# A gated recurrence ahead of a folded feed-forward block: the order of the opening transfers and jobs is written anew

## The chip, the core and the metric

The kernel runs on one core of one Trainium2 chip. The metric is the device time of one execution in microseconds (us); several executions of one kernel are summed up by their median. Inside the core five engines work side by side, each through its own queue in strict order: TensorE (PE in the profile), VectorE (DVE), ScalarE (ACT), GpSimd (POOL) and SyncE (SP). SP only issues transfers (DMA). PE writes to PSUM, a small memory of banks; the others read it there.

## The reference, cut to what matters

There are 4 sequences of 5824 tokens with 256 channels, 23296 tokens in all. A gated linear recurrence runs along each sequence, and its output goes through a feed-forward block that multiplies two projections.

```python
log_a = 8.0 * sigmoid(r_gate) * log(clip(sigmoid(a_param)))
a_t   = exp(log_a)
norm  = sqrt(maximum(1.0 - a_t * a_t, 1e-06))
h     = a_t[:, t] * h + norm * sigmoid(i_gate) * x      # along t; y[:, t] = h
a, b  = y @ w1, y @ w2                                  # 256 -> 1024 each
out   = ((a * b) @ w3) @ w_out                          # 1024 -> 1024 -> 256
```

The kernel folds w3 @ w_out once into one matrix of 1024 x 256 (`wp_sb`), since nothing lies between the two products.

## The kernel before, in words

The tokens are cut into 47 chunks: two of 256 tokens, 44 of 512 and one of 256. The two matrices of the up projections (w1, w2) and the folded matrix stay in SBUF. Every piece of work of a chunk is a named step, and the list `ORDER` gives all 2464 steps in one sequence; each step issues its instructions on one engine's queue. An engine takes its own steps in that order and waits, at each, until what the step reads is there and the buffer that it writes is free. So the list, and the sets that assign steps to engines, fix the schedule; there is no planner at run time.

The steps of chunk c, by letter, with the lines of the kernel before:

- `r c`, `i c`, `x c` load the three inputs (L136, on SP). `Lw1.k`, `Lw2.k`, `Lwo.k`, `Lw3.k` load a piece of 512 KB of a weight (L354, on SP) and `Cw...` casts it to bf16 (L361 to L363: POOL, or ACT and DVE for the members of `W_ACT` and `W_DVE`).
- `R c` and `I c` are the tanh of the two gates (L145 to L154, ACT). The sigmoids are computed from it. `p c` adds one (L159, POOL), `t c.half` multiplies by x (L175, L178).
- `V c` and `U c` turn the results so that channels lie on partitions. They are done by PE with 4 or 8 small transposes into PSUM (L185) for chunks in `TURN_R` and `TURN_U`, and by a transposing transfer on SP (L196) for the others.
- `d c.cb` is the exponential of one half of the channels (L207, ACT), `s c.cb` its square (L215, L217: ACT, DVE or POOL by set), `q c` the square root (L221, ACT). Root and exponential use different tables on ACT, so a change between them puts an ACT_TABLE_LOAD into ACT's queue.
- `g c` gates (L229 or L232, DVE), `h c.cb` is the scan along time (L249, DVE) and needs the chunk before, `y c` casts to bf16 (L258, POOL or ACT).
- `a c.mp.q` and `b c.mp` are the up projections of 128 and 256 hidden columns (L269, PE). `c c.mp.q` copies a from PSUM (L283 on DVE, L285 on ACT), `m c.mp` multiplies a and b (L297, DVE).
- `D c.j` is the folded down projection of 128 tokens (L308, PE), `e c.j2` copies it from PSUM, `o c.j2` stores it (L327, SP).
- `Ft`, `Fc`, `Fm`, `Fe` with an index 0 to 7 transpose a piece of w3, copy it, multiply it with w_out and copy the result to `wp_sb` (L368, L285 or L283, L379, L414 or L416). No `D` can begin before the last `Fe`.
- `W n` issues two matmuls on the identity matrix whose result nobody reads (L263, PE). There are 16 of them.

Buffers come from rings: `RINGS` gives the number of slots of each, and a step that takes a slot waits for the last reader of its former content. The PSUM ring "po" has 4 slots and serves `V`, `U`, `a`, `D`, `Ft` and `Fm`; the ring "pb" has 2 and serves `b` and `W`. Weight pieces are staged in the slots of the rings "a" and "nrm", 6 each, that also hold d's and s's results.

The transfers of SP run through one queue. In the trace at most eight of them are open: each has one of eight semaphores, and SP waits for the landing of the transfer that had it before.

The last 1961 of the 2464 steps stand in the same order before and after the change, so the change lies in the work up to about `b7.2`, the up projection of chunk 7.

Of the kernel before, what the change touches and what calls it, by code (L numbers as in the profile page):

```python
# [22 lines left out]
def kernel(  # L23
# [12 lines left out]
    nc = tc.nc  # L36
# [12 lines left out]
    CT = 512  # L49
    sizes = [256, 256] + [CT] * 44 + [256]  # L50
    assert sum(sizes) == NTOK
# [28 lines left out]
    TURN_R = {0, 1, 2, 3, 4, 7, 12}  # L80
    TURN_U = {0, 1, 2, 3, 4, 5, 6, 7}
    DV_TIMES = {0, 1}
    DV_PLUS = set()
    DV_HALF = {(2, 0)}
    DV_SQUARE = {(0, 0), (1, 0), (10, 0)}
    AC_SQUARE = {(1, 1), (2, 0), (2, 1), (3, 0), (4, 0), (4, 1), (6, 0), (8, 1), (9, 1), (11, 0), (11, 1), (12, 1),
        (13, 0), (13, 1), (14, 0), (14, 1), (15, 1)}
    DV_CAST = set()
    AC_CAST = {4}
    DV_COPY = {(0, 0, 0), (0, 1, 0), (0, 1, 1), (0, 3, 0), (1, 1, 0), (1, 1, 1), (1, 2, 0), (1, 2, 1), (1, 3, 0), (2,  # L90
        0, 1), (2, 1, 0), (2, 1, 1), (2, 3, 0), (3, 0, 1), (3, 2, 0), (3, 2, 1), (4, 0, 0), (4, 1, 0), (4, 2, 0), (4, 2,
        1), (5, 1, 1), (5, 2, 1), (6, 2, 0), (6, 2, 1), (6, 3, 1), (7, 0, 0), (7, 1, 1), (7, 3, 0), (7, 3, 1), (8, 1, 0),
        (8, 2, 0), (9, 1, 0), (9, 1, 1), (9, 2, 1), (10, 0, 0), (10, 1, 0), (10, 1, 1)}
    DV_EVAC = {(1, 0), (2, 0), (3, 1), (5, 1), (9, 0), (9, 1)}
    FOLD_ACT = {('c', 7), ('e', 0), ('e', 1), ('e', 2), ('e', 3), ('e', 7)}
    W_ACT = {('w2', 0), ('w3', 6)}
    W_DVE = {('w1', 1)}
    STAGE = {'w1': ['a', 'a'], 'w2': ['nrm', 'nrm'], 'wo': ['a', 'nrm'], 'w3': ['a', 'nrm', 'a', 'nrm', 'a', 'nrm',
        'a', 'nrm']}
    CASTING = set()  # L100
# [60 lines left out]
    def times(c, half):  # L161
        n = sizes[c] // P
        fused = c in DV_TIMES
        if half == 0 or fused:
            T["u", c] = ring(gates, [P, NCB, 4, P], BF16, name="u_t", tag="u")
# [34 lines left out]
    def decay(c, cb):  # L200
        w = sizes[c]
        if cb == 0:
            T["a", c] = ring(held, [P, NCB, CT], F32, name="a_t", tag="a")
        a, pr = T["a", c][:, cb, :w], T["pr", c][:, cb, :w]
        if long_rows(c):
            a, pr = in_time(a), turned(pr)
        nc.scalar.activation(out=a, in_=pr, func=AF.Exp, scale=la4[:, cb:cb + 1], bias=la4[:, cb:cb + 1])  # L207

    def square(c, cb):
        w = sizes[c]  # L210
        if cb == 0:
            T["n", c] = ring(held, [P, NCB, CT], F32, name="nrm", tag="nrm")
        n, a = T["n", c][:, cb, :w], T["a", c][:, cb, :w]
        if (c, cb) in AC_SQUARE:
            nc.scalar.activation(out=n, in_=a, func=AF.Square)  # L215
        else:
            (nc.vector if (c, cb) in DV_SQUARE else nc.gpsimd).tensor_mul(out=n, in0=a, in1=a)  # L217

# [17 lines left out]
    def scan(c, cb):  # L236
        w = sizes[c]
        if cb == 0:
            T["h", c] = ring(ypool, [P, NCB, CT], F32, name="h_t", tag="h")
        h, a, n = (T[key, c][:, :, :w] for key in "han")  # L240
        if cb == 0:
            for b in range(1, B):
                if 0 < b * S - starts[c] < w:
                    nc.vector.memset(a[:, :, b * S - starts[c]:b * S - starts[c] + 1], 0.0)
# [42 lines left out]
    def copy(c, mp, q):  # L287
        w = sizes[c]
        if q == 0:
            T["sa", c, mp] = ring(ffn, [P, 2, CT], BF16, name="sa", tag="sa")  # L290
        copy_to((c, mp, q) in DV_COPY, T["sa", c, mp][:, q, :w], T["pa", c, mp, q][:, :w])

    def product(c, mp):
        w = sizes[c]
        if mp == 0:
            T["g", c] = ring(ffn, [P, KD, CT], BF16, name="g_t", tag="g")
        nc.vector.tensor_mul(out=T["g", c][:, 2 * mp:2 * mp + 2, :w], in0=T["sa", c, mp][:, :, :w],  # L297
                             in1=T["pb", c, mp][:, :, :w])

    def down(c, j):  # L300
        if c == NCH - 1:
            T["po_last", j] = po = ring(psum_o, [P, D], F32, name="po", tag="po")
        else:
            if j % 2 == 0:
                T["po", c, j // 2] = ring(psum_o, [P, 2, D], F32, name="po", tag="po")
# [19 lines left out]
    def store(c, j2):  # L325
        t0 = starts[c] + 2 * j2 * P
        nc.sync.dma_start(out=out[t0:t0 + 2 * P, :].rearrange("(j p) c -> p j c", p=P),  # L327
                          in_=T["ot", c, j2])

# [88 lines left out]
    def last(c):  # L418
# [20 lines left out]
    ORDER = """  # L439
        r0 r1 E A3. A0. A1. i1 R1 R0 W3 V1 I1 V0 W13 W12 A2. W9 d1.0 d1.1 s1.0 i0 W15 I0 x0 t0.1 W14 d0.0 s0.0 s1.1  # L440
        d0.1 s0.1 q0 x1 t1.1 Lw1.0 r3 Lw2.0 r2 q1 R3 Lw1.1 i2 W11 U0 g0 h0.0 Lw2.1 Cw1.0 W10 W2 U1 W0 W7 R2 W4 h0.1
        Lw3.2 x2 g1 y0 W8 Lwo.0 Cw2.0 a0.1.0 a0.1.1 h1.0 c0.1.0 h1.1 a0.0.0 a0.0.1 V2 c0.1.1 d2.0 c0.0.0 W6 y1 b0.0
        c0.0.1 d2.1 I2 Cw1.1 a1.0.1 a1.0.0 b0.1 a1.1.0 a0.2.0 c1.0.0 c1.0.1 Cw2.1 p2 a0.2.1 Cw3.2 m0.0 m0.1 c1.1.0
        Lwo.1 b1.0 m1.0 t2.0 r4 W1 c0.2.0 a1.1.1 a0.3.0 t2.1 Cwo.0 W5 c1.1.1 Ft2 c0.2.1 a1.3.0 s2.0 b1.1 c0.3.0 b0.2
        U2 a1.3.1 s2.1 Cwo.1 i3 Fc2 V3 x3 Lw3.0 q2 Lw3.1 i4 Lw3.4 m1.1 c1.3.0 Fm2 R4 g2 h2.0 h2.1 d3.0 Lw3.7 c1.3.1
        m0.2 d3.1 Lw3.5 Fe2 a1.2.0 a0.3.1 b1.2 a1.2.1 I3 c0.3.1 V4 s3.0 d4.0 d4.1 b0.3 y2 c1.2.0 Cw3.0 c1.2.1 m1.2
        a2.0.0 a2.1.0 b1.3 m0.3 a2.2.0 b2.0 m1.3 a2.2.1 c2.0.0 Lw3.3 a2.0.1 s4.0 c2.2.0 s3.1 p3 t3.0 c2.1.0 Cw3.1 Ft0
        c2.0.1 c2.2.1 Fc0 m2.0 Cw3.4 b2.1 I4 s4.1 q4 r7 t3.1 a2.3.0 a2.1.1 Fm0 b2.2 p4 Cw3.5 c2.1.1 Ft4 c2.3.0 m2.1
        Fe0 Ft1 a2.3.1 U3 Lw3.6 q3 Fc4 c2.3.1 Fc1 Fm4 Cw3.7 b2.3 Ft5 g3 Fe4 Fc5 Ft7 x4 Cw3.3 R7 r5 h3.0 h3.1 Fm1 Fm5
        Fc7 Fe5 Ft3 Fm7 Fe1 Cw3.6 V7 Fe7 y3 Ft6 Fc3 d7.0 d7.1 Fc6 m2.2 Fm3 i6 r6 a3.1.0 Fe3 R5 Fm6 a3.1.1 c3.1.0  # L450
        c3.1.1 t4.0 Fe6 t4.1 i7 i5 x5 U4 a3.0.0 R6 D0.0 a3.0.1 D0.1 I6 c3.0.0 e0.0 m2.3 g4 a3.3.0 a3.2.0 b3.0 h4.0
        h4.1 b3.1 c3.0.1 m3.0 D1.0 a3.3.1 D1.1 I5 c3.3.0 y4 V5 r8 m3.1 a3.2.1 V6 b3.2 I7 e1.0 c3.2.0 c3.2.1 c3.3.1
        b3.3 m3.2 m3.3 p5 a4.0.1 r9 a4.1.0 d5.0 d5.1 R8 d6.0 s6.0 s7.0 d6.1 p6 t5.0 p7 x6 x7 o0.0 a4.0.0 i10 V8 D2.0
        D2.1 c4.0.0 c4.1.0 b4.0 r10 o1.0 s5.0 s5.1 R9 s6.1 c4.0.1 s7.1 e2.0 m4.0 a4.2.0 a4.2.1 q7 V9 c4.2.0 a4.1.1
        c4.2.1 b4.1 t5.1 b4.2 c4.1.1 U5 a4.3.0 i8 o2.0 m4.1 D3.0 r11 t6.0 t6.1 U6 q5 q6 g5 h5.0 h5.1 c4.3.0 m4.2 i9 g6
        d8.0 a4.3.1 D3.1 D2.2 D2.3 b4.3 c4.3.1 d9.0 e3.0 y5 a5.1.0 t7.0 s8.0 b5.0 m4.3 e2.1 R10 d8.1 a5.0.0 a5.0.1
        h6.0 h6.1 a5.2.0 c5.1.0 D4.0 c5.0.0 c5.0.1 I8 m5.0 x8 a5.1.1 D4.1 c5.2.0 o3.0 I9 b5.1 a5.2.1 c5.1.1 b5.2 m5.1
        c5.2.1 R11 e4.0 p8 y6 m5.2 r12 I10 t7.1 a5.3.0 a6.0.0 U7 V10 c5.3.0 c6.0.0 d9.1 x10 r13 D3.2 g7 D3.3 e3.1
        a6.0.1 x9 t8.0 t8.1 a6.1.0 d10.0 d10.1 o2.1 V11 a6.1.1 a5.3.1 h7.0 h7.1 s9.0 c6.0.1 s9.1 c6.1.0 b6.0 R13 o4.0
        a6.2.1 a6.2.0 c5.3.1 c6.1.1 y7 m6.0 b5.3 s8.1 U8 D4.2 b6.1 a7.0.0 p9 p10 m5.3 t9.0 c6.2.0 b6.2 c6.2.1 R12 m6.1  # L460
        a6.3.0 q8 q9 D4.3 a6.3.1 c7.0.0 m6.2 c6.3.0 e4.1 t9.1 b6.3 c6.3.1 t10.0 t10.1 m6.3 V12 a7.0.1 g8 x11 h8.0 h8.1
        b7.0 a7.1.0 s10.0 d12.0 d12.1 c7.1.0 c7.0.1 D6.0 D6.1 m7.0 a7.2.0 D5.0 a7.1.1 D5.1 V13 d13.0 s13.0 i11 I11
        e6.0 o3.1 d11.0 y8 d11.1 e5.0 r15 c7.1.1 a7.2.1 b7.1 c7.2.0 c7.2.1 b7.2 U9 U10 i13 i12 r14 o4.1 x13 d13.1 o6.0
        a7.3.0 a7.3.1 a8.0.1 o5.0 m7.1 m7.2 R15 I13 a8.0.0 c8.0.0 b7.3 c8.0.1 c7.3.0 D6.2 c7.3.1 m7.3 p11 b8.1 s11.0
        D6.3 b8.0 a8.1.0 D5.2 D5.3 g9 h9.0 s10.1 s12.0 t11.0 i16 s11.1 R14 h9.1 e6.1 I12 c8.1.0 q10 p13 a8.1.1 c8.1.1
        m8.0 V15 q11 p12 y9 e5.1 m8.1 a8.3.0 D7.0 D7.1 V14 i15 o5.1 o6.1 r16 t13.0 t11.1 U11 r19 x12 a8.2.0 c8.2.0 g10
        h10.0 h10.1 c8.3.0 e7.0 y10 a8.2.1 d15.0 r17 b8.2 a8.3.1 b9.0 a9.0.0 c8.2.1 t13.1 m8.2 o7.0 x15 s15.0 a9.0.1
# [142 lines left out]
```

## Time and profile before

| what | value |
|---|---|
| time, median of 3 executions | 514.76 us (514.51 to 515.69) |
| profiled execution, its own time | 514.32 us |
| its span, first to last instruction | 512.4 us |
| PE, ACT, DVE, POOL busy | 500.2, 465.6, 428.0, 312.8 us |
| last PE work ends, by the timeline | about 509.3 us |
| first `a` matmul (chunk 0) | 14.01 us |
| first `a` matmul of chunk 2 | 28.35 us |
| granted TensorE clock over the span | 1.00 |

A row of the timeline reads: start, duration, engine, line, operation, output and inputs, shape, how many, and in brackets how long the engine had been idle and who ended that. Matmuls overlap, so the rate of PE is read from start to start: 512 columns take 216 ns, 256 take 109 ns and 128 take 56 ns in the steady part of this trace. For the other engines too the distance from start to start of a run of instructions is a little smaller than one's duration.

### The profile page before, as it was taken

The numbers are of one execution on the slowest core, as the hardware profiler recorded it, in microseconds if no ns is written. First come the engines' busy times: TensorE is split into PE (matmuls) and PEld (weight loads), VectorE is DVE, ScalarE is ACT, GpSimd is POOL, SyncE is SP. The second block draws the span as 40 slices with busy tenths as digits, with TensorE's granted clock in tenths as the row PEclk, the third lists the DMA queues.
The fourth block names the chain that finished last, engine by engine and source line by source line (L and its number), as shares of the span: only waits on it lengthen the run. The fifth ranks groups of instructions, "written<-read, shape, count | busy, mean of one in ns | idle before, by whom it ended". The sixth has DMA issues, their size and how long they took to land.

```text
span 512.4 us, 8840 instructions
## 1 busy us (share of the span) xinstructions
PE 500.2 (98%) x3171; PEld 308.7 (60%) x3225; DVE 428.0 (84%) x414; ACT 465.6 (91%) x720; POOL 312.8 (61%) x271
## 2 busy tenths in 40 slices
PE   7899999999999999999999999999999999999997
PEld 3667565665565566556666556565566655656566
DVE  4899999999999879878878799878878697959762
ACT  7999999999999999999999999998998979888543
POOL 2683958546638945966685983957647569580200
PEclk9999999999999999999999999999999999999999
DMA  8998999999999998797999995898695895253112
GB/s 301 409 415 264 326 320 265 263 290 318 319 230 278 276 291 265 191 323 151 294 287 306 276 302 156 238 229 248 186 266 138 240 299 158 101 156 71 57 57 104
DMA packets 177280, 123.80 MB, mean 242 GB/s; under 512 B 86354, under 2 KB 172884, under 8 KB 177236
## 3 DMA queue, kind: packets, MB, share of 16 engines
q1 hardware_dynamic: 177232, 123.23, 84.1%
q8 instruction: 25, 0.41, 0.3%
q14 instruction: 19, 0.16, 0.1%
q10 hardware_dynamic: 4, 0.00, 0.0%
HBM read 78.91 MB, written 23.86 MB: 201 GB/s over the span
## 4 chain that ended last, share of the span: by engine, by line
PE 90%; ACT 4%; DMA 3%; issue 1%; SPq 1%; DVE 1%; ACTq 0%; DVEq 0%
PE po L308 30%; PE pb L269 29%; PE pa L269 28%; DMA r_t<-in_r_gate_dram 2%; DMA i_t<-in_i_gate_dram 1%; PE pw L379 1%; ACT sa L285 1%; PE ptr L185 1%; SPq L136 1%; PE ptw L368 1%; DVE h_t L249 0%; ACT th_r L145 0%; ACT a_t L207 0%; ACT ot L285 0%; ACT L154 0%
## 5 line engine op out<-in xcount | busy, mean ns | idle before, releaser
L297 DVE TENSOR_TENSOR g_t<-sa,pb 128x1024 bf16<-128x1024 bf16 (+1 forms) x188 | 218.9, 1181 | 63.0 <-PE pb L269 30.0
L269 PEld LDWEIGHTS <-w_sb 128*128 128x128 bf16 x1504 | 146.2, 98 | 146.9 <-issue 4.7
L285 ACT CAST sa<-pa 128x512 bf16<-128x512 f32 (+1 forms) x339 | 182.5, 588 | 26.7 <-PE pa L269 18.4
L269 PE MATMUL pa<-y_t,w_sb 128*128 128x512 bf16 (+1 forms) x721 | 185.8, 372 | 3.5 <-ACT sa L285 2.5
L269 PE MATMUL pb<-y_t,w_sb 128*128 128x512 bf16 (+1 forms) x729 | 182.5, 372 | 1.5
L308 PE MATMUL po<-wp_sb,g_t 128*128 128x256 bf16 x1456 | 177.7, 273 | 0.3
L308 PEld LDWEIGHTS <-g_t 128*128 128x128 bf16 x1456 | 142.4, 98 | 40.2 <-issue 0.5
L258 POOL CAST y_t<-h_t 128x1024 bf16<-128x1024 f32 (+1 forms) x46 | 51.1, 1112 | 142.1 <-DVE h_t L249 142.1
L178 POOL TENSOR_TENSOR u_t<-i_t,x_t 128x512 bf16<-128x512 f32 (+1 forms) x89 | 120.5, 1371 | 3.8 <-issue 1.7
L249 DVE TENSOR_TENSOR_SCAN h_t<-a_t,h_t,nrm 128x512 f32<-128x512 f32 (+1 forms) x92 | 119.7, 1331 | 1.9
L217 POOL TENSOR_TENSOR nrm<-a_t 128x512 f32<-128x512 f32 (+1 forms) x74 | 80.9, 1111 | 13.6 <-ACT a_t L207 10.7
L207 ACT ACTIVATE a_t<-rt,la 128x512 f32<-128x512 bf16 (+1 forms) x80 | 64.2, 821 | 0.0
L159 POOL TENSOR_SCALAR i_t<-i_t 128x1024 f32<-128x1024 f32 (+1 forms) x45 | 53.1, 1184 | 18.0 <-ACT i_t L154 18.0
L285 ACT COPY ot<-po 128x512 f32<-128x512 f32 (+1 forms) x85 | 49.6, 590 | 12.3 <-PE po L308 12.0
L232 DVE SCALAR_TENSOR_TENSOR nrm<-nrm,ut 128x1024 f32<-128x1024 f32 (+1 forms) x39 | 53.4, 1370 | 5.2 <-ACT nrm L221 5.2
L154 ACT ACTIVATE i_t<-i_t 128x1024 f32<-128x1024 f32 (+1 forms) x47 | 49.2, 1049 | 0.4 <-DMA i_t<-in_i_gate_dram 0.4
L221 ACT ACTIVATE nrm<-nrm 128x1024 f32<-128x1024 f32 (+1 forms) x47 | 48.3, 1040 | 0.2
L147 ACT ACTIVATE th_r<-r_t 128x1024 bf16<-128x1024 f32 (+1 forms) x40 | 42.6, 1065 | 0.0
L283 DVE CAST sa<-pa 128x512 bf16<-128x512 f32 (+1 forms) x37 | 21.8, 617 | 1.1 <-PE pa L269 0.9
L221 ACT ACT_TABLE_LOAD x17 | 21.8, 1283 | 0.3
L263 PE MATMUL warm<-ident 128*128 128x512 bf16 x32 | 11.1, 490 | 0.0
L215 ACT ACTIVATE nrm<-a_t 128x512 f32<-128x512 f32 (+1 forms) x17 | 10.7, 649 | 0.1
(57 smaller groups left out, 126.8 us busy)
## 6 DMA issues: line engine op xcount, KB each, us to landing
out_dram<-ot SPq DMA_DIRECT2D x90, 256.0 KB, 3.5
r_t<-in_r_gate_dram SPq DMA_DIRECT2D x44, 512.0 KB, 5.2
i_t<-in_i_gate_dram SPq DMA_DIRECT2D x44, 512.0 KB, 5.5
x_t<-in_x_dram SPq DMA_DIRECT2D x44, 512.0 KB, 5.3
wf<-in_moe_w_dram SPq DMA_DIRECT2D x12, 512.0 KB, 10.1
wf<-in_moe_w_out_dram SPq DMA_DIRECT2D x2, 512.0 KB, 10.3
r_t<-in_r_gate_dram SPq DMA_DIRECT2D x3, 256.0 KB, 2.9
i_t<-in_i_gate_dram SPq DMA_DIRECT2D x3, 256.0 KB, 4.1
```

The costliest lines, as they stand in the source:

```text
L159: (nc.vector if c in DV_PLUS else nc.gpsimd).tensor_scalar(t, t, 1.0, 1.0, op0=ALU.add, op1=ALU.mult)
L178: (nc.vector if (c, half) in DV_HALF else nc.gpsimd).tensor_mul(out=u, in0=t, in1=xt)
L207: nc.scalar.activation(out=a, in_=pr, func=AF.Exp, scale=la4[:, cb:cb + 1], bias=la4[:, cb:cb + 1])
L217: (nc.vector if (c, cb) in DV_SQUARE else nc.gpsimd).tensor_mul(out=n, in0=a, in1=a)
L221: nc.scalar.activation(out=T["n", c][:, :, :w], in_=T["n", c][:, :, :w], func=AF.Sqrt, scale=-1.0, bias=1.0)
L232: nc.vector.scalar_tensor_tensor(out=T["n", c][:, :, :w], in0=T["n", c][:, :, :w], scalar=1e-3, in1=T["pu", c][:, :, :w], op0=ALU.max, op1 ...
L249: nc.vector.tensor_tensor_scan(h[:, cb, :], a[:, cb, :], n[:, cb, :], init, ALU.mult, ALU.add)
L258: eng.tensor_copy(out=T["y", c][:, :, :w], in_=T["h", c][:, :, :w])
L269: nc.tensor.matmul(out=dst[:, :w], lhsT=w_sb[:, cb, m * P:(m + 1) * P], rhs=T["y", c][:, cb, :w], start=(cb == 0), stop=(cb == NCB - 1))
L285: nc.scalar.copy(out=dst, in_=src_ps)
L297: nc.vector.tensor_mul(out=T["g", c][:, 2 * mp:2 * mp + 2, :w], in0=T["sa", c, mp][:, :, :w], in1=T["pb", c, mp][:, :, :w])
L308: nc.tensor.matmul(out=po, lhsT=T["g", c][:, k, j * P:(j + 1) * P], rhs=wp_sb[:, k, :], start=(k == 0), stop=(k == KD - 1), skip_group_che ...
```

## The change: what it does

All steps stay, none is added; 503 of them are put in another order, some change the engine.

- Transfers: the opening order `r0 r1 i1 i0 x0 x1` becomes `r1 i0 r0 x0 i1 x1`. Then `Lw1.0 r3 Lw2.0 r2 Lw1.1 i2 Lw2.1 Lw3.2 x2` becomes `Lw1.0 r2 i2 Lw2.0 r3 Lw1.1 x2 Lw2.1 Lw3.2`.
- `U6` leaves `TURN_U`: PE's 8 transposes of chunk 6 become one transposing transfer on SP.
- Up to `b7.2`, ACT has 11 copies (`c`) fewer and DVE 11 more; one cast of y goes from ACT to POOL; `t2.0` from DVE to POOL; the casts of `w1.1`, `w2.0`, `w2.1`, `wo.0`, `w3.1` and `w3.6` change engine among ACT, DVE and POOL. Squares and fold copies move singly.
- The steps `W` stand elsewhere. Ahead of the first `a` of chunk 0 there were 13, now 12; between `U1` and that `a` there were 4, now 8.
- The helpers no longer assume that half 0 of a pair comes first: the first to arrive takes the buffer. This changes no instruction. `store` and `evac` take the width of a pair from a new helper, with the same result for every chunk that uses them.

```diff
     TURN_R = {0, 1, 2, 3, 4, 7, 12}
-    TURN_U = {0, 1, 2, 3, 4, 5, 6, 7}
+    TURN_U = {0, 1, 2, 3, 4, 5, 7}
     DV_TIMES = {0, 1}
-    DV_HALF = {(2, 0)}
-    DV_SQUARE = {(0, 0), (1, 0), (10, 0)}
+    DV_HALF = set()
+    DV_SQUARE = {(0, 0), (0, 1), (1, 1), (10, 0)}
...
-    AC_CAST = {4}
+    AC_CAST = set()
...
-    W_ACT = {('w2', 0), ('w3', 6)}
-    W_DVE = {('w1', 1)}
+    W_ACT = {('w2', 1), ('w3', 1), ('wo', 0)}
+    W_DVE = {('w2', 0)}
...
-        r0 r1 E A3. A0. A1. i1 R1 R0 W3 V1 I1 V0 W13 W12 A2. W9 d1.0 d1.1 s1.0 i0 W15 I0 x0 t0.1 W14 d0.0 s0.0 s1.1
-        d0.1 s0.1 q0 x1 t1.1 Lw1.0 r3 Lw2.0 r2 q1 R3 Lw1.1 i2 W11 U0 g0 h0.0 Lw2.1 Cw1.0 W10 W2 U1 W0 W7 R2 W4 h0.1
-        Lw3.2 x2 g1 y0 W8 Lwo.0 Cw2.0 a0.1.0 a0.1.1 h1.0 c0.1.0 h1.1 a0.0.0 a0.0.1 V2 c0.1.1 d2.0 c0.0.0 W6 y1 b0.0
...
+        A3. r1 i0 r0 x0 i1 x1 E A0. A1. A2. R1 I0 R0 W10 W13 V1 V0 W2 d1.0 d1.1 d0.0 s1.0 t0.1 s1.1 s0.0 d0.1 I1 t1.1
+        s0.1 q0 W14 U0 U1 W6 W11 W8 W3 W9 W1 W0 q1 W5 g0 h0.0 h0.1 g1 h1.0 Lw1.0 Cw1.0 y0 a0.0.1 c0.0.1 h1.1 r2 i2 R2
+        Lw2.0 Cw2.0 V2 a0.1.0 W12 a0.1.1 a0.0.0 W15 r3 Lw1.1 x2 Lw2.1 I2 d2.0 d2.1 y1 s2.1 p2 s2.0 R3 q2 Cw1.1 t2.0
+        t2.1 Cw2.1 c0.1.0 c0.1.1 b0.1 c0.0.0 m0.1 a1.1.1 a1.0.1 b0.0 a1.0.0 a1.1.0 b1.1 c1.1.1 m0.0 c1.0.1 c1.1.0
+        c1.0.0 m1.1 b1.0 a0.2.1 c0.2.1 a0.2.0 c0.2.0 a1.2.0 a1.3.1 c1.2.0 m1.0 a1.2.1 c1.3.1 c1.2.1 b0.2 m0.2 V3 U2
+        Lw3.2 Cw3.2 a0.3.0 Ft2 Lwo.1 Cwo.1 r4 Lwo.0 Lw3.4 Lw3.0 i3 Lw3.1 Lw3.7 x3 d3.1 d3.0 Fc2 R4 g2 c0.3.0 h2.1 h2.0
+        Cwo.0 W7 W4 a0.3.1 b1.2 b1.3 a1.3.0 V4 Fm2 y2 m1.2 Lw3.3 Lw3.5 Lw3.6 r7 i4 r5 r6 x4 i5 i6 b0.3 d4.1 s3.1 Fe2
...
     def times(c, half):
...
-        if half == 0 or fused:
+        if ("u", c) not in T:
             T["u", c] = ring(gates, [P, NCB, 4, P], BF16, name="u_t", tag="u")
```

## The prediction

> **What bounds the kernel now.** I read the page first: its busy times, its slices and the chain that ended last.
>
> ```profile
> PE 500.2 (98%) x3171; PEld 308.7 (60%) x3225; DVE 428.0 (84%) x414; ACT 465.6 (91%) x720; POOL 312.8 (61%) x271
> ...
> PE   7899999999999999999999999999999999999997
> ...
> PE 90%; ACT 4%; DMA 3%; issue 1%; SPq 1%; DVE 1%; ACTq 0%; DVEq 0%
> ```
>
> PE is on the chain for 90% of the span, and only the first slices lie below 9. Then I took the timeline of PE, which shows how the first 30 us are spent.
>
> ```profile
> 5.68 5.33 PE L263 MATMUL warm<-ident 128*128 128x512 bf16 x12
> 10.80 0.43 PE L185 MATMUL ptr<-ident,u_t 128*128 128x128 bf16 x4
> 11.07 1.03 PE L263 MATMUL warm<-ident 128*128 128x512 bf16 x4
> ...
> 14.01 1.03 PE L269 MATMUL pa<-y_t,w_sb 128*128 128x256 bf16 x8
> ...
> 18.95 0.38 PE L269 MATMUL pa<-y_t,w_sb 128*128 128x256 bf16 x2 [1.10 <-ACT sa L285]
> ...
> 26.50 0.38 PE L269 MATMUL pa<-y_t,w_sb 128*128 128x256 bf16 x2 [1.24 <-ACT sa L285]
> ```
>
> Three things are to be seen. The first real work starts at 14.01. Up to 26.5 there are two waits (1.10 and 1.24) and three more `W` steps. And the clock matters: 12 warm matmuls take 5.33, 0.427 each from start to start; after 10.89 four take 1.03 with the last one's tail, 0.216 each. From 28.6 to the end the starts of the matmuls follow one another without a gap over 0.2 us that isn't just a missing record. So nothing can be won behind 28.6 except PE work itself. What can be won is in the opening.
>
> The stretches show how near the other engines are to full there (PE, PEld, DVE, ACT, POOL).
>
> ```profile
> 10.00:30.00 20.00, 17.43 (x145) 11.83 (x145) 17.04 (x31) 19.61 (x30) 11.69 (x12) 1.00 1.04 412
> 30.00:50.00 20.00, 19.89 (x188) 14.99 (x188) 17.89 (x25) 18.88 (x27) 13.21 (x13) 1.00 0.96 336
> 50.00:98.80 48.80, 48.48 (x315) 29.89 (x320) 47.49 (x51) 48.52 (x69) 34.26 (x31) 1.00 1.08 285
> ```
>
> **What the Trainium skill says.** (1) "TensorE: Matmul & The Clock Gate", Part 1: PE begins at half clock and gets the full one after a window of about 3.4 us of sustained work; the window runs freely, so the moment differs between executions. The trace agrees: half speed until 10.89, 5.2 us after the steady work began at 5.68. (2) "ScalarE: Activation LUTs", What ACT_TABLE_LOAD costs: 1283 ns plus a drain. Here the load takes 1.28 and the next instruction starts 1.30 after it (8.89 to 10.19). (3) "SBUF — State Buffer", SBUF: two separate sides: a DVE instruction with two SBUF inputs and a GpSimd instruction shut each other out. The trace has a sign of it: `t2.1` on POOL took 1.71 beside `t2.0` on DVE, later ones 1.27. (4) "DMA: Bandwidth & Descriptors", Where 436 GB/s comes from: a ceiling of 435 GB/s. In the trace the landings of 512 KB follow each other every 1.25 to 1.36 us up to 44 us, 420 GB/s at best, in the order of issue. So a landing is known from the place in the order.
>
> **Part 1, the first transfers and ACT.** The landings in the trace are 3.28, 4.05, 5.58, 6.23, 6.87 and 7.52; the new order puts r1, i0, r0, x0, i1, x1 on them. ACT: R1 at 3.30, I0 at 4.07, R0 at 5.61, then from start to start 0.5 for R and 0.45 for each of four exponentials (6.14, 1.00 for two, less the tail): I1 starts at 7.92 and ends at 8.54. Table load 1.30, so q0 runs from 9.86 to 10.43 (before: 10.19). Both squares of chunk 0 are now on DVE, the second behind `t1.1` (8.56 to 9.25), ending at 9.7, in time. `g0` before started at 11.34, because `U0` sat behind 12 half-speed warm matmuls until 11.2. Now `U0` is done at 8.8, and `g0` starts at 10.46. Gating and scans took 11.34 to 13.28, the cast of y 0.06 + 0.62: y0 is ready at 13.08 instead of 13.96, a gain of 0.88 if PE is free.
>
> **Part 2, the warm matmuls.** PE is not free. `U1` needs `t1.1` and ends at 9.72; behind it stand 8 `W` steps, 16 matmuls, before `a0.0.1`. At full clock they take 16 x 0.216 = 3.46 and end at 13.18; at half clock 16 x 0.427 = 6.83 and end at 16.55. If the clock opens at O, the end is O + (16 - (O - 9.72)/0.427) x 0.216. Steady work begins at 6.27 (`V0`), with one gap of 0.5 before `U1`. If the gap is forgiven, O lies in 9.7 to 13.1 (3.4 to 6.8 after the start); if not, in 12.7 to 16.1. O = 10.89 gives 13.75, 12.7 gives 14.65, 14.3 gives 15.44. I take 14.7 for the start of `a0.0.1`, against 14.01: **a loss of 0.7**. DVE waits with it, since its copy `c0.0.1` now stands ahead of `h1.1`, `Cw2.0` and with them of y1 and the first b; ACT waits too, since `V2` follows `a0.0.1` and `d2.0` needs it.
>
> **Part 3, from there to chunk 2.** In the new order DVE has no hole between `c0.0.1` and the end of `h2.0`: 14 copies of 256 columns x 0.33, one scan 0.64, the weight cast 0.65, 5 products x 0.62, two gatings 1.19, two scans 2.45 = 12.65 (all from start to start of the rows of before). It starts 0.4 after `a0.0.1`, y2 adds 1.1: `a2.0.0` comes 14.2 after `a0.0.1`. The other chain, POOL's `s2.1`, `p2`, `Cw1.1` (three x 1.04) and `t2.0`, `t2.1` (two x 1.27) from the end of `d2.1`, ends within 0.2 of it. In the kernel before `a2.0.0` stood at 28.35, with `b1.3` (0.44) still to do, which the new order has done by then, and a gap of 0.23: comparable 29.0, 15.0 after its first `a`. **Gain 0.8**: the two waits and the `W` steps of before, of which the new order keeps a part. x2 lands at 17.7 instead of 20.2, but `t2.0` is behind `Cw1.1` on POOL until about 19 and is slower there than on DVE; the earlier landing alone is worth nothing.
>
> **Part 4, U6.** Eight transposes leave PE: 8 x 0.056 = **0.45 gained**, as PE is dense there. The transfer is issued behind the store `o2.1` on SP, at about 67; transposes landed about 5 us after their issue (46.72 to 51.59). `g6` needs it at about 73. Should it be late, `h6` and then chunk 6 wait, a us per us.
>
> **Part 5, the balance up to b7.2.** DVE gets 11 copies more (7 of 256 columns), less single items: 3.0 us more; ACT 2.3 less. Before, DVE had in the stretch from 10 to 98.8 6.4 idle, ACT 1.8. So DVE has 3 to 4 left, which is enough on average, but every `m` frees one of two "pb" slots and every copy one of four "po" slots, and PE waits where one is late. From below nothing, from above what a queue without slack lost at the start, 1.2. I take **a loss of 0.4**.
>
> **Sum** against the profiled execution (514.32, span 512.4): -0.7 + 0.8 + 0.45 - 0.4 = 0.15 faster, span 512.25, time 514.2. The median shown, 514.76, lies 0.44 above that execution, and its clock may have opened early; I add half of it: **514.4 us**.
>
> **The likeliest (0.46)**: within 0.2% (about 1.03 us, what a measurement can tell from no change), 513.7 to 515.8. **Rival, faster (0.28)**: the clock opens as early as before, at 10.9 or sooner, the start is at 13.75 or below, and the slots hold: 0.26 + 0.8 + 0.45 - 0.2 = 1.3 faster, 513.2. For it speaks that in the new order PE would be busy for 86% of 7.48 to 10.89, the window that opened the clock before; against it that the kernel before was busy for about 76% of 4.07 to 7.48, one window earlier, and the clock stayed at half. **Rival, slower (0.15)**: the clock opens only when the 16 warm matmuls are nearly through, and the start is at 16.5: -2.5 + 0.8 + 0.45 - 0.4 = 1.7 slower, 516.2. It decides from a start of about 15.9, an opening at 15.2. **Rival, slower (0.11)**: DVE, with 3.0 more, is the bound between 28 and 57, and PE waits there for 1.5 or more: 515.8. That the earlier landings change nothing is part of the likeliest.
>
> The range that holds 8 in 10 is 512.8 to 516.4: the low end is an early clock and no stall (1.5 gained), the high end a late clock with 0.4 of stalls and the median above its profile. Chances: faster 0.28, same 0.46, slower 0.26.
>
> **What would show it.** Part 1: `g0` near 10.5 and the cast of y near 12.5. Part 2: the spacing of the 16 warm matmuls, 0.427 or 0.216, and the first `a` at 14.7, later than 14.01. Part 3: `a2.0.0` near 28.9. Part 4: no `U6` on PE and `g6` not waiting. Part 5: PE without gaps from there, DVE above 17.9 busy in 30 to 50. I am wrong if the first `a` is at 13.1, if r0 in the third place lands well before 5.58, or if PE shows waits for DVE behind 30.

## The result, and the profile after

The changed kernel takes 517.97 us (median of 15 executions, 515.96 to 519.65); on the same chip the kernel before takes 515.65 (15 executions, 514.51 to 516.51). The ratio is **1.0047, 95% interval 1.0034 to 1.0061: slower**. The forecast was no change, 514.4, with a range up to 516.4. The profiled execution takes 516.24, the fourth quickest of the 15, with a span of 514.4, 2.0 more span than before.

The page of the changed kernel, busy times, PE's slices and the chain that ended last:

```profile
PE 499.7 (97%) x3163; PEld 308.2 (60%) x3217; DVE 433.4 (84%) x423; ACT 464.7 (90%) x712; POOL 313.6 (61%) x270
...
PE   7899989999999999999999999999999999999997
```

PE has 0.5 us less to do, as the 8 transposes of chunk 6 promised, but one slice has fallen to 8, the sixth, from 64 to 77 us. On the chain that ended last PE holds 76% where it held 90%, and ACT 12% where it held 4%. So the loss is behind the opening, where I expected nothing but 0.4. The stretch from 62 to 80 us says the same; first of the kernel before (start:end, length, then PE, PEld, DVE, ACT, POOL busy, clock, share and GB/s of DMA):

```profile
62.00:80.00 18.00, 17.95 (x134) 12.01 (x133) 17.71 (x19) 17.97 (x26) 12.03 (x12) 1.00 1.05 323
```

then of the changed kernel:

```profile
62.00:80.00 18.00, 16.25 (x118) 11.14 (x119) 16.29 (x18) 16.35 (x25) 8.93 (x9) 1.00 1.14 290
```

All four engines lose 1.4 to 3.1 us in the same stretch, so none of them is full there. The waits of the changed kernel between 60 and 125 us (engine, line, waited for: us in total, times, longest) name it:

```profile
PE pa L271 <- ACT sa L287: 2.0, 2, 1.6
ACT a_t L208 <- DMA rt<-th_r: 1.6, 1, 1.6
DVE nrm L233 <- DMA ut<-u_t: 1.5, 1, 1.5
ACT th_r L148 <- DMA r_t<-in_r_gate_dram: 1.2, 1, 1.2
```

Three of the four wait for a transfer: `V9` (rt), `U6` (ut) and `r14`. PE's longer wait of 1.64, for ACT's copies, follows from the first of them. The chain from 57 to 75 us gives it step by step (start, length, what):

```profile
62.40 1.06 ACT th_r L148
63.45 0.03 ACT sa L287
63.48 6.69 DMA rt<-th_r
70.17 0.02 issue
70.19 0.02 ACT a_t L208
...
70.91 1.04 ACT th_r L148
71.95 0.70 ACT a_t L208
72.66 1.17 ACT sa L287 x3
```

`R9` runs, SP issues `V9` at 63.48, it lands 6.69 later, `d9.0` can start at 70.19 only, and behind it on ACT stand `R10`, `d8.1` and the copies `c5.2.1`, `c5.2.0` that free PE's "po" slots. The timeline of PE has the first of two stalls, and the opening:

```profile
9.48 3.83 PE L265 MATMUL warm<-ident 128*128 128x512 bf16 x16
13.14 0.38 PE L271 MATMUL pa<-y_t,w_sb 128*128 128x256 bf16 x2
...
26.99 1.03 PE L385 MATMUL pw<-wo_sb,w3t 128*128 128x256 bf16 x8 [0.31 <-ACT wo_sb L367]
27.86 0.60 PE L271 MATMUL pb<-y_t,w_sb 128*128 128x256 bf16 x4
...
73.18 0.59 PE L271 MATMUL pa<-y_t,w_sb 128*128 128x512 bf16 x2 [1.64 <-ACT sa L287]
```

A second stall follows at 111 to 112 (0.37 and 0.66): `R11` runs at 88.69 on ACT instead of 75.31, so `V11` and with it `r14` are late (105.73 instead of 102.08).

Why is `V9` late? SP's own timeline:

```profile
43.84 1.34 SPq L197 DMA_TRANSPOSE rt<-th_r  x1
...
47.49 1.26 SPq L137 DMA_DIRECT2D x_t<-in_x_dram  x2
...
58.48 8.13 SPq L197 DMA_TRANSPOSE rt<-th_r  x2
...
67.32 1.30 SPq L197 DMA_TRANSPOSE ut<-u_t  x1
```

The first row is `V5`. SP had reached it at 37.2 and stood there until `R5` had run on ACT. SP stood at `V5` as long in the kernel before (40.1 to 46.7), but there `i7` and `x5` were issued ahead of it (34.60 and 38.23; they landed at 44.94 and 47.66). The new order puts these two behind it (`x6` was behind it before too): x5 lands at 54.79, i7 at 63.39. The DMA engines have a hole in both kernels, from 45 to 51 us before and from 43 to 48 here, but now two loads of 512 KB, 1.25 to 1.4 each, that had landed before or in the hole are behind it, and the transfers behind them with them. The third row shows SP busy for 8.13 us with issuing `V8` and `V9` (4.85 and 3.13; before, 1.24 and 1.58), though what `V8` waited for was there at 57.5.

ACT's order has a part in it too. Before, `V9` was issued at 60.11 and `d9.0` came to its turn at 68.19, 8.1 later; here it is issued at 63.48, since `R9` now stands behind the square roots, and the turn of `d9.0` comes at 68.58, 5.1 later.

**The account of the profiled pair.** The opening gives 0.7 (29.0, the comparable place of before, against 28.30), `U6` 0.45; PE's gaps behind 50 us cost about 3.0 more than before, read from start to start (1.8 between 71 and 73, 0.3 at 86, 1.1 at 110 to 112, less 0.2 that the kernel before has too); some 0.15 is not placed. That is the 2.0 of the spans.

### The profile page after: what moved, and what is told of

It is laid out like the page before. It is cut to its first block, busy times and chain, and to the rows that moved or that the text cites. A ratio compares the mean times of both kernels' runs of the same rounds, so it can differ in the third digit from the quotient of the medians.

```text
span 514.4 us, 8824 instructions
## 1 busy us (share of the span) xinstructions
PE 499.7 (97%) x3163; PEld 308.2 (60%) x3217; DVE 433.4 (84%) x423; ACT 464.7 (90%) x712; POOL 313.6 (61%) x270
## 4 chain that ended last, share of the span: by engine, by line
PE 76%; ACT 12%; DVE 4%; issue 4%; DMA 2%; SPq 0%; ACTq 0%; DVEq 0%
PE po L313 26%; PE pb L271 25%; PE pa L271 24%; ACT sa L287 3%; ACT a_t L208 2%; DMA rt<-th_r 1%; DVE g_t L299 1%; ACT nrm L222 1%; DVE h_t L251 1%; ACT th_r L148 1%; ACT ot L287 1%; DMA x_t<-in_x_dram 1%; PE warm L265 1%; ACT i_t L155 1%; ACT L222 1%
## 5 line engine op out<-in xcount | busy, mean ns | idle before, releaser
L287 ACT CAST sa<-pa 128x512 bf16<-128x512 f32 (+1 forms) x328 | 177.4, 592 | 27.3 <-PE pa L271 18.0
L260 POOL CAST y_t<-h_t 128x1024 bf16<-128x1024 f32 (+1 forms) x47 | 52.6, 1119 | 146.4 <-DVE h_t L251 144.1
L251 DVE TENSOR_TENSOR_SCAN h_t<-a_t,h_t,nrm 128x512 f32<-128x512 f32 (+1 forms) x92 | 121.1, 1344 | 2.3 <-DVE nrm L233 0.5
L218 POOL TENSOR_TENSOR nrm<-a_t 128x512 f32<-128x512 f32 (+1 forms) x72 | 79.3, 1117 | 11.0 <-ACT a_t L208 8.2
L233 DVE SCALAR_TENSOR_TENSOR nrm<-nrm,ut 128x1024 f32<-128x1024 f32 (+1 forms) x40 | 55.8, 1396 | 6.3 <-ACT nrm L222 4.9
L287 ACT COPY ot<-po 128x512 f32<-128x512 f32 x86 | 50.2, 591 | 11.7 <-PE po L313 11.5
L285 DVE CAST sa<-pa 128x512 bf16<-128x512 f32 (+1 forms) x48 | 27.0, 595 | 1.4 <-PE pa L271 1.1
L216 ACT ACTIVATE nrm<-a_t 128x512 f32<-128x512 f32 x18 | 11.3, 647 | 0.1
L265 PE MATMUL warm<-ident 128*128 128x512 bf16 x32 | 9.8, 449 | 0.0
```

The source lines that it names most:

```text
L233: nc.vector.scalar_tensor_tensor(out=T["n", c][:, :, :w], in0=T["n", c][:, :, :w], scalar=1e-3, in1=T["pu", c][:, :, :w], op0=ALU.max, op1 ...
L251: nc.vector.tensor_tensor_scan(h[:, cb, :], a[:, cb, :], n[:, cb, :], init, ALU.mult, ALU.add)
L287: nc.scalar.copy(out=dst, in_=src_ps)
```

## The experiments

The ratio is always to the kernel before on the same chip; "the changed kernel" is 1.0047. Its `ORDER` is the base of all edits, where nothing else is said.

**First round: is one step of ACT wrongly placed?** Four edits of single steps.

`e1_d9_behind`: the waiting exponential stands behind the copies.
```diff
-... D2.1 V9 d9.0 R10 d8.1 ... s8.1 c5.0.1 I9
+... D2.1 V9 R10 d8.1 ... s8.1 c5.0.1 d9.0 I9
```


> The changed kernel with one step of ACT moved: d9.0 stands behind c5.0.1 instead of ahead of R10. Theory A (late transposing transfers): in the changed kernel d9.0 waits 1.60 for the transfer V9 and holds up the copies c5.2.1 to c5.1.1, for which PE waits 1.64 at 71.5. With d9.0 behind them the PE wait goes, and the time falls by 1.2 to 1.6 us against the changed kernel (ratio to before about 1.0018). Theory B (ACT and DVE are simply full there, the waits only move): the time stays within 0.4 us of the changed kernel. Theory C (the clock of PE opens later in most executions, and that is the whole difference): the time stays, and the wait at 71.5 is no cause.

Measured 517.86, 1.0059 [1.0037, 1.0081]. `d9.0` no longer stands in the way, but its neighbours do: `d8.0` waits 1.3 for `V8`, `g6` waits 2.6 for `U6`, PE 2.04 at 77 to 79. The whole queue is late, not one step.

`e2_r9_early`: `R9` ahead of `s6.0`, so that `V9` can be issued sooner.
```diff
-... x7 s6.0 t5.0 ... h5.0 R9 c4.1.0
+... x7 R9 s6.0 t5.0 ... h5.0 c4.1.0
```


> The changed kernel with R9 moved on ACT ahead of s6.0, as the kernel before has it on the near side of the change of tables, so that V9 can be issued right behind V8. Theory A: V9 lands before 68.5 instead of at 70.17, d9.0 doesn't wait, PE's wait of 1.64 goes; 1.2 to 1.6 us less than the changed kernel. If instead the backlog of loads in the queue is what makes V9 late, V9 still lands at 69 or later and less than 0.6 us comes back. Theory B and C: no change beyond 0.4 us.

Measured 517.87, 1.0065 [1.0043, 1.0086]. Now `R9` itself waits 1.0 for r9, V9 still lands at 69.28, and PE waits 1.40 at 61, earlier than in the changed kernel.

`e3_r11_early`: `R11` directly behind `R13`.
```diff
-... e3.1 R13 q8 ... q9 R11 d10.0
+... e3.1 R13 R11 q8 ... q9 d10.0
```


> The changed kernel with R11 moved on ACT from behind q9 to behind R13. V11, which stands on SP ahead of r15, U9, U10, i13, i12 and r14, then doesn't hold them up. Theory A: V11 is issued near 88 instead of 91.2, r14 lands near 103 instead of 105.73, R14 doesn't wait its 1.18, and PE's waits of 0.37 and 0.66 at 111 go; 0.8 to 1.2 us less than the changed kernel. Theory B and C: no change beyond 0.4 us.

Measured 518.18, 1.0059 [1.004, 1.0078]. The stall at 111 is gone, as meant; in this profile the first one was 2.63 and cost more than itself (last section).

`e4_both`: the edits of e2 and e3.

> The changed kernel with both moves, R9 ahead of s6.0 and R11 behind R13. Theory A: the two stalls go, 2.2 to 2.8 us less than the changed kernel, so equal to the kernel before or up to 0.7 us under it (ratio 0.9985 to 1.0005). Theory C: still 1.5 us or more above the kernel before, since the opening is untouched.

Measured 518.3, 1.0067 [1.0046, 1.0089]. None of these rearrangements on ACT helps: the reason lies ahead of it.

**Second round: SP's queue, and which part of the order.**

`e5_x_ahead`: two loads go ahead of the transfer that SP stands at.
```diff
-... y4 V5 a3.2.1 ... R8 d6.1 x6 x5 r9
+... y4 x6 x5 V5 a3.2.1 ... R8 d6.1 r9
```


> The changed kernel with two loads moved on SP: x6 and x5 stand ahead of V5 instead of behind V6. Theory D: SP stands at V5 from 37.2 to 43.8 (V5 needs R5 on ACT), the transfer engines run dry at 45.5, and all later transfers, V8, V9 and U6 among them, come 2.5 us late; the moves of R9 and R11 couldn't help since r9 and V8 are late themselves. Then x6 and x5 land near 48, V9 lands at or before 68.5 instead of 70.17, U6 isn't waited for, PE's wait at 71.5 falls under 0.4, and the time falls by 1.3 to 2 us against the changed kernel (ratio to before 1.001 to 1.003). Theory B (ACT and DVE are full, whatever the transfers): within 0.5 us of the changed kernel, with a PE wait of 1 us or more somewhere between 57 and 78.

Measured 516.45, 1.0033 [1.0016, 1.005]. x5 lands at 48.05 instead of 54.79, V9 at 69.01, 4.04 behind its issue instead of 6.69, and PE's stall at 73 of 1.64 is gone; what remains is about 0.5 at 77, 0.7 at 111 and 0.4 at 130. The span is no shorter for it (514.5), since the first `a` of this execution came at 14.63, 1.5 later. Unlike e1 to e4, this edit takes the stall away in its profile and doesn't move it. By time alone it can't be told from the changed kernel (the intervals overlap).

It isn't the change undone: `x6` goes ahead of where it stood before, and `i7` stays behind. And SP now stands elsewhere. It waits 6.0 us, until 56.8, to issue the store `o0.0` (the second row), whose tile ACT has to copy first; `i10`, `i7` and `r10` are behind it, i7 lands at 63.13 against 63.39, and the DMA engines move 88 GB/s between 55 and 58 us, where in the changed kernel they moved 384.

```profile
50.25 0.50 SPq L137 DMA_DIRECT2D i_t<-in_i_gate_dram  x1
56.84 0.39 SPq L333 DMA_DIRECT2D out_dram<-ot  x1
```

`e6_x_r9`: the same, and `R9` early.

> The changed kernel with x6 and x5 ahead of V5 and R9 ahead of s6.0. Theory D: r9 lands near 53.5 instead of 56.1, R9 doesn't wait, V9 lands near 66.5; the time is that of the kernel with the two loads alone or up to 0.5 us less. Theory B: R9 ahead of the square roots makes c4.2.0 late by 1 us, PE waits for it near 59, and the time is 0.5 us or more above that of the two loads alone.

Measured 516.99, 1.0032 [1.0023, 1.0042]: nothing beyond e5.

`h1_open_new`: the first 251 steps as in the change, then the old order and engines.

> The opening of the changed kernel up to Fm6 (its first 251 steps with their engines), then the steps that are left in the order and on the engines of the kernel before. Theory D (the loss lies behind the opening, in the order of SP): faster than the kernel before by 0.3 to 0.9 us, no PE wait over 0.5 between 50 and 120. Theory C (the opening and the clock make the loss): slower than before by 1 us or more.

`h2_rest_new`: the old opening of 245 steps, then the new order and engines.

> The opening of the kernel before up to Fm6, then the steps that are left in the order and on the engines of the changed kernel. Theory D: SP stands at V5 here too, so PE waits 1 to 3 us between 57 and 78 and about 1 us near 111; slower than before by 2 to 3 us, like the changed kernel. Theory C: within 0.8 us of the kernel before.

Measured 515.94, 1.0015 [1.0002, 1.0028], and 519.05, 1.008 [1.0065, 1.0095]. The new opening doesn't gain; the new rest loses more than the whole change does, so the larger part of the loss is in the rest. The seam costs something in both (a gap of 0.9 at 48 to 49 in h1), so they don't add up to the change.

**Third round: the opening, and U6 alone.**

`e7_v3`: e5 and
```diff
-... m1.0 a1.2.1 c1.3.1 c1.2.1 b0.2 m0.2 V3 U2
+... m1.0 V3 a1.2.1 c1.3.1 c1.2.1 b0.2 m0.2 U2
```


> The changed kernel with x6 and x5 ahead of V5 (as in the earlier run of that pair) and, beside it, V3 moved on PE from behind b0.2 to ahead of a1.2.1. Theory (the exponential table's load waits until V3 has ended, because it belongs to d3.1 and starts only when d3.1's input is there): V3 ends near 20.6 after a first a of 13.1, the load runs from about 20.7 to 22.0, d3.1 starts near 22.0 instead of 22.70, and a2.0.0 follows the first a by 14.3 to 14.6 instead of 15.16; the time falls by 0.6 to 0.8 against the run with x6 and x5 alone, to about 515.8. Rival (y2 on POOL, behind h2.0 on DVE, ends as late as the table chain): a2.0.0 stays 15.0 or more behind the first a and the time stays at 516.4.

Measured 516.33, 1.0024 [1.0013, 1.0035]. In the changed kernel ACT's table load starts when `V3` has ended (21.34):

```profile
21.41 1.28 ACT L208 ACT_TABLE_LOAD   x1 [1.18 <-issue]
22.70 1.45 ACT L208 ACTIVATE a_t<-ptr,la 128x512 f32<-128x512 bf16 x2
24.04 1.01 ACT L287 COPY w3t<-ptw 128x1024 bf16<-128x1024 bf16 x1
24.93 1.07 ACT L146 ACTIVATE th_r<-r_t 128x1024 bf16<-128x1024 f32 x1
25.89 1.05 ACT L367 CAST wo_sb<-wf 128x1024 bf16<-128x1024 f32 x1
```

In e7, whose first `a` is 1.11 later and whose `V3` ends at 21.57:

```profile
21.63 1.28 ACT L208 ACT_TABLE_LOAD   x1 [0.30 <-issue]
22.93 1.45 ACT L208 ACTIVATE a_t<-ptr,la 128x512 f32<-128x512 bf16 x2
25.07 1.01 ACT L287 COPY w3t<-ptw 128x1024 bf16<-128x1024 bf16 x1 [0.70 <-PE ptw L374]
25.98 1.06 ACT L146 ACTIVATE th_r<-r_t 128x1024 bf16<-128x1024 f32 x1
26.94 1.04 ACT L367 CAST wo_sb<-wf 128x1024 bf16<-128x1024 f32 x1
```

Counted from the first `a` the load is 0.89 earlier, as expected of it. But ACT now waits 0.70 for `Ft2` on PE, and the cast of `Cwo.0` ends 13.73 behind the first `a` instead of 13.80. `a2.0.0` follows at 15.08, not 14.3 to 14.6. The theory that the table load sets this stretch has fallen; the rival's number came, but y2, ready at 14.36, isn't what `a2.0.0` waits for. What stands ahead of `a2.0.0` is read off below.

`e8_warm`: e5, and 4 of the 16 warm matmuls moved forward.
```diff
-    WARM = [2] * 16
+    WARM = [2, 2, 2, 2, 2, 2, 3, 2, 1, 2, 2, 2, 2, 2, 2, 2]
-... W10 W13 V1 V0 W2 ... W14 U0 U1 W6 W11 W8 W3
+... W10 W13 V1 W6 V0 W2 ... W14 U0 W8 U1 W11 W3
```


> The changed kernel with x6 and x5 ahead of V5, and with 4 of its 16 warm matmuls behind U1 moved forward: three (W6) into PE's wait between V1 and V0, one (W8) between U0 and U1. Theory (the moment at which the clock opens sets the first a, and it opens late in some executions because PE stands still for 1.3 and 0.35 us ahead of the run of warm matmuls): PE is busy without a hole from 2.3 on, the clock opens before 10 in the profile, the first a starts at 12.8 to 13.3, set by y0, and the timed median falls by about 0.8 against the run with x6 and x5 alone, to 515.6, with less spread. Rival (the moment is free of what PE did before): the first a is late in some executions as before, and the median stays at 516.4.

Measured 516.14, 1.0016 [0.9999, 1.0032]. PE's timeline in e8:

```profile
4.61 1.48 PE L265 MATMUL warm<-ident 128*128 128x512 bf16 x3
...
9.71 2.75 PE L265 MATMUL warm<-ident 128*128 128x512 bf16 x12
13.33 0.38 PE L271 MATMUL pa<-y_t,w_sb 128*128 128x256 bf16 x2 [0.87 <-POOL y_t L260]
```

The twelve run at full clock and the first `a` waits for y0, no longer for PE. The clock opened at 7.12 here, and at 6.75, 5.60 and 7.13 in the three later runs with this edit; in the eight profiles of the new opening without it that record the moment it opened between 9.22 and 12.68. The place of the warm matmuls sets it. The spread of the times did not shrink (514.67 to 518.94), so that half of the expectation missed.

`e9_all`: e5, e7, e8 and e3 together.

> The changed kernel with x6 and x5 ahead of V5, V3 ahead of a1.2.1, the four warm matmuls moved forward, and R11 behind R13 on ACT. If the four causes are separate, the gains add up: 516.45 less 0.7 (table load), less 0.8 (clock), less 0.7 (PE's wait at 111) gives about 514.3, level with the kernel before or 0.1% faster. If one wait only makes way for the next, the time stays at 515.5 to 516.5 and the profile shows new waits of PE between 40 and 130.

Measured 515.5, **1.0006 [0.999, 1.0021]**: of the loss of 2.4 us at most 1.1 is left (the medians on this chip, 515.50 and 514.58, lie 0.9 apart). No share of one edit is resolved by time; together they are.

The stall isn't ruled out, though. In e9's own profile (516.32, among its slower executions) V9 lands at 70.09 again, and PE waits 0.95 at 73 and 2.5 us in all between 50 and 135. Its waits between 40 and 135 us have the same two lines as the changed kernel:

```profile
PE pa L271 <- ACT sa L287: 2.0, 4, 1.0
ACT a_t L208 <- DMA rt<-th_r: 2.0, 2, 1.0
```

Over the six profiles with `x6` and `x5` ahead (e5 to e9 and f2 below) PE's waits between 50 and 135 us sum to 0.5 to 2.5, mean 1.2; over the six without (the changed kernel, e1 to e4 and f1 below) to 0.8 to 3.9, mean 2.7.

`e10_u6`: the kernel before, with one part of the change alone.
```diff
-    TURN_U = {0, 1, 2, 3, 4, 5, 6, 7}
+    TURN_U = {0, 1, 2, 3, 4, 5, 7}
```


> The kernel before with one part of the change: chunk 6's gated input is turned by a transposing DMA, at its old place in the order. Prediction's part 4: eight transposes leave PE, 0.45 less, 514.4 where the kernel before has 514.9, if g6 doesn't wait or its wait stays on DVE. Theory of the queue: U6 is issued near 65.0, behind r11, and lands near 70, while g6 stands at 69.3 on DVE; a wait of DVE of up to 1 us, and the transfers of i9, x8 and V10 behind it half a us later; PE waits for at most 0.5, so the time lies between 514.4 and 515.0. If a transposing DMA is issued as slowly as V8 was in the changed kernel (4.8 us), g6 waits 3 or more and the time is 516 or above.

Measured 517.35, 1.0037 [1.0022, 1.0052]. The part that I had booked as a gain of 0.45 costs about 1.9 when it stands alone. Its profile is of a quick execution (515.82) and has one wait of PE, 0.48 at 76.9, so it doesn't show where the 1.9 goes.

**Fourth round: what is it about U6?**

`f4_unread`: the kernel before, `U6` on PE, and the transfer beside it into a tile that nobody reads.
```diff
+    def turn_both(c):
+        turn_dma(c, "pu", "u")
+        turn_pe(c, "pu", "u")
```


> The kernel before, with U6 turned on PE as it was, and the transposing DMA of U6 issued beside it into a tile that nobody reads (its content is of no use). If U6's cost comes from the transfer (SP's queue, the transfers behind it), the time is 517 or more, 0.45 above the run with U6 by DMA alone less what g6 cost. If it comes from g6's wait or from g6's reading of SBUF, the time is that of the kernel before within 0.1%, 514.3 to 515.2.

Measured 514.97, 0.9997 [0.9982, 1.0012]: the transfer itself costs nothing. What costs is that `g6` reads what it brings.

`f3_g6_late`: e10, with 1.2 us more for the landing.
```diff
-... m4.2 i9 g6 d8.0 ... s8.0 b5.0 m4.3 e2.1
+... m4.2 i9 d8.0 ... s8.0 b5.0 m4.3 g6 e2.1
```


> The kernel before with U6 by DMA, and g6 moved on DVE from ahead of m4.3 to behind it, which gives U6's landing about 1.2 us more. If U6's cost comes from g6 waiting for a landing with no slack, most of it goes and the time is 514.5 to 515.5. If it comes from the transfer on SP's queue or from g6 reading SBUF beside POOL, the time stays at 516.5 to 517.5.

Measured 515.58, 1.0007 [0.9995, 1.002]: most of the cost is gone. The landing came at 69.71 in e10, at 69.19 in f4 and at 71.78 in f3, with issues at 65.41, 64.61 and 64.95. So it takes 4.3 to 6.8 us, and `g6` at 69.3 to 69.9 had no slack at all. In f3's profile, with its late landing, `g6` waits in spite of the move, and PE 1.64 at 77:

```profile
69.79 1.22 DVE L297 TENSOR_TENSOR g_t<-sa,pb 128x1024 bf16<-128x1024 bf16 x1 [0.31 <-PE pb L269]
71.86 1.22 DVE L232 SCALAR_TENSOR_TENSOR nrm<-nrm,ut 128x1024 f32<-128x1024 f32 x1 [0.85 <-DMA ut<-u_t]
```

`f1_u6_pe`: the changed kernel with `U6` back on PE, behind `b5.2`.

> The changed kernel with one part undone: chunk 6's gated input turned on PE again (behind b5.2), all else as in the change. PE has 0.45 more work. Theory Q (the order of SP's queue from V5 on carries the loss, U6 is a small part): V9 still lands near 70, d9.0 waits 1 us or more, PE waits 1.5 at 73 and the time is 517.5 to 518.5. Theory U (U6 by DMA carries most of the loss, as it costs 0.37% alone): the time falls to 515.5 to 516.5.

Measured 517.23, 1.0047 [1.0036, 1.0059]. Nothing comes back, so in the changed kernel `U6` is not what the loss hangs on: `d9.0` waits 1.6 for `V9` here too.

`f2_all_u6_pe`: e9 with `U6` on PE.

> The changed kernel with x6 and x5 ahead of V5, V3 ahead of a1.2.1, four warm matmuls forward, R11 behind R13, and U6 on PE again. Theory Q: no better than the run with the same edits and U6 by DMA, 515.5 to 516, since PE gets 0.45 more. Theory U: 1 to 2 below it, 513.5 to 514.5, which would be 0.1 to 0.2% faster than the kernel before.

Measured 515.36, 1.0004 [0.9994, 1.0014], as e9. PE waits for another engine for at most 0.5 at a time between 50 and 135 us.

**Last: one cause planted, and the best version.**

`g2_x5_behind`: the kernel before, with two loads moved behind `V5` and `V6` on SP.
```diff
-... t4.1 i7 i5 x5 U4 ... V5 r8 m3.1 a3.2.1 V6 b3.2
+... t4.1 i5 U4 ... V5 r8 m3.1 a3.2.1 V6 x5 i7 b3.2
```


> The kernel before, with x5 and i7 moved on SP from ahead of V5 to behind V6 and nothing else. Theory Q (V5 holds SP until R5 has run on ACT, the DMA engines run dry and everything behind lands later): x5 lands near 55 instead of 47.7, V8 and V9 land 2 us or more later than 63 and 67, PE waits for 1 us or more between 55 and 80, and the ratio is 1.002 to 1.006. Rival (the order of the transfers is not enough, it needs the new order of the engines' work too): PE waits for less than 0.3 us, ratio 0.999 to 1.001.

Measured 520.14, 1.0094 [1.0074, 1.0114], beyond what either theory gave. PE's timeline:

```profile
60.01 1.03 PE L269 MATMUL pb<-y_t,w_sb 128*128 128x512 bf16 x4
63.68 1.99 PE L269 MATMUL pa<-y_t,w_sb 128*128 128x512 bf16 x6 [2.65 <-ACT sa L285]
```

and ACT's:

```profile
56.25 1.06 ACT L154 ACTIVATE i_t<-i_t 128x1024 f32<-128x1024 f32 x1 [3.29 <-DMA i_t<-in_i_gate_dram]
```

Two loads behind `V5` are enough to slow the old order; nothing else was touched. The link is i7, though, which `I7` meets on ACT at 53, and not x5 as I had said. In the changed kernel `I7` stands later on ACT and doesn't wait. The run shows that loads behind `V5` can slow the kernel, and not what x5 or i7 cost in the changed order.

`g1_open_mended`: the new opening with the edits of e7 and e8, then everything as before.

> The first 251 steps of the changed kernel with V3 ahead of a1.2.1 and four warm matmuls forward, and then everything in the order and on the engines of the kernel before. With the new opening as it stands the ratio was 1.0015. V3 gave 0.09% and the warm matmuls 0.17% beside x6 and x5, so if the terms add up the ratio is 0.9985 to 0.9995, about 514.4 where the kernel before has 515.0; PE has no wait over 0.5 us behind 50. Rival (the old order behind needs the old landings: chunk 4 to 6 are late after the new opening): a wait of PE of about 1 us near 48, as in the run with the new opening alone, and a ratio of 1.000 to 1.001.

Measured 514.64, 0.9992 [0.9982, 1.0003]: the best of all, but not to be told from the kernel before. The rival's wait near 47 is in its profile (0.76 for POOL's u).

## Why the prediction was wrong, by its own steps

**Part 1, right.** `g0` starts at 10.25 (said 10.46), y0 is ready at 12.86 (13.08). What it lacked is that the third landing varies: r0 came between 4.76 and 6.59 in the 14 profiles with this opening.

**Part 2, mechanism right, size off.** I took 14.7 for the first `a`; the profile has 13.14, since the clock opened at 9.89 and the gap ahead of `U1` was forgiven. Over ten profiles with this opening and unmoved warm matmuls it lies between 13.01 and 15.00, mean 13.76. The base was off too: six profiles with the old opening have 13.09 to 14.01, mean 13.55, so 14.01 was a late one. The loss is 0.2, not 0.7; that this execution gained 0.87 is luck. The first `a` at 13.1 was one of my signs of being wrong, and it came on the good side.

**Part 3, the failed term is "`a2.0.0` comes 14.2 after `a0.0.1`".** It is 15.16 (15.08 to 15.32 in all 14). The sum over DVE and y2 was right: y2 ends 14.37 after the first `a`. But in PE's queue `Fm2` and `b0.3` stand ahead of `a2.0.0`, and `Fm2` starts at 26.99 because ACT's cast `Cwo.0` ends at 26.94: 0.87 and 0.44 from there are 28.30. I had costed DVE's and POOL's chains and not ACT's. The table load that waits for `V3` is in that chain, but e7 shows that it alone doesn't set it. Against the comparable 15.0 of before, the gain of 0.8 is a loss of 0.16 in this pair; the later start of before hid it.

**Part 4, the issue and the landing right, the time of need wrong.** The transfer was issued at 67.32 and landed at 71.63, 4.3 later. But `g6` stood ready at 70.27, not at 73, and waited 1.48; in the kernel before it had run at 69.34. "About 5 us" was also one figure for what takes 4.3 to 6.8 in the runs above, so a need at 73 would have been met or missed by the draw.

**Part 5, the step that decided.** "A loss of 0.4" was sized by how full DVE is, and it is about 3.0 in the profile. DVE did get fuller from 30 to 50 (18.79, said above 17.9) and PE stayed at 19.89 there, so that did no harm:

```profile
30.00:50.00 20.00, 19.89 (x183) 14.54 (x183) 18.79 (x28) 19.31 (x26) 14.49 (x14) 1.00 0.94 327
```

From 50 to 98.8 DVE is busy for 46.19, less than before's 47.49. The waits that ACT and DVE have there are for transfers, and PE waits for ACT's copies (1.64) more than for DVE (0.66 at 112). I had followed SP's queue only as far as `U6`, not the two loads that the order moves behind `V5`, nor the time from the issue of `V9` to the turn of `d9.0`. The rival "DVE is the bound" had the sign and over half of the size, by a mechanism that the profile excludes: PE has no wait for DVE between 28 and 57. The new account is borne by e5's profile, by e9, which brings the ratio to 1.0006, and by g2, where planting raises it to 1.0094.

What it doesn't show is how the loss divides. e9 also betters the opening, and by the ratios of h1 and g1, 1.0015 and 0.9992, its two edits there may be worth 1.2 us of the 2.1 that e9 gains, an estimate across two chips. The two loads alone gave back 0.7 (e5), within the noise, and left SP standing at `o0.0`. So late transfers as the cause of the stalls are shown; that the place of `x5` and `i7` is the main reason for their lateness is argued. Why SP takes up to 4.8 us to issue `V8` stays open too.

## What to carry to other kernels

In a queue that serves all transfers, one that waits for another engine's result holds back every load behind it: put the loads that need nothing ahead of it, and cost a new order by the queue of SP as by those of the engines. A step moved from PE to a transfer is paid for in slack: give it the longest landing seen, not the median. A single profile of an opening is one draw; compare several before a difference of 1 us is believed.

## What the runs showed of the hardware

**The clock halves again after a wait of 2.6 us.** In e3 PE was busy for 0.39 of 72.00 to 75.00, and from 76.27 the clock was at half for 3.4 us; in g2 the same followed a wait of 2.65, from 64.45:

```profile
64.45:67.86 3.41, 3.41 (x10) 1.21 (x8) 2.02 (x4) 3.40 (x5) 3.41 (x3) 0.50 1.14 244
```

Each time this adds about 1.7 us of PE work to the stall: in g2, 2.8 and 1.7 make up the 4.4 by which its span is longer. The Trainium skill, "TensorE: Matmul & The Clock Gate", Part 1, gives an idle window of about 3.4 us as the condition; here waits of 2.63 (e3) and 2.65 (g2) were enough, while 2.29 in e4 and 2.04 in e1 were not.

Unprofiled executions seem to have it too. A stretch of 3.4 us at half clock takes 0.003 off the mean clock of the span. In 5 of the 15 executions of the changed kernel that mean is 0.997, and their median is 519.21; the other ten have 517.23. All four executions of g2 read 0.997. Of 175 executions of the kernel before, measured beside the experiments, 15 read 0.997. So about 0.7 of the 2.3 us between the medians may be the clock's answer to a long wait.

**A gating that reads SBUF instead of PSUM can lose 1.1 to GpSimd.** The Trainium skill, "SBUF — State Buffer", SBUF: two separate sides, says that a DVE operation with two SBUF inputs and a GpSimd operation that reads SBUF exclude each other for a whole instruction. e10's profile agrees. Its DVE timeline:

```profile
69.90 2.34 DVE L232 SCALAR_TENSOR_TENSOR nrm<-nrm,ut 128x1024 f32<-128x1024 f32 x1
```

and POOL's:

```profile
69.89 1.27 POOL L178 TENSOR_TENSOR u_t<-i_t,x_t 128x512 bf16<-128x512 f32 x1
71.13 2.02 POOL L217 TENSOR_TENSOR nrm<-a_t 128x512 f32<-128x512 f32 x1
```

`g6` begins 0.01 after `t7.0` and ends 1.1 behind it; `s8.0`, else 1.03, ends 0.9 behind `g6`. Beside the same `t7.0` but from PSUM, `g6` took 1.22 in the kernel before; from SBUF with POOL idle it took 1.22 in f3 and 1.23 in the changed kernel. So it is the neighbour together with the second SBUF input that costs, and turning a tile by DMA also changes what its reader shares. f3 moved `g6` away from both, the early landing and `t7.0`, so how e10's cost divides between them is open.
